# Attention by hash buckets and a gated feed-forward block on one core: aligned v blocks, full-height scores, a new order of loads, and one more pair turned by TensorE

## The chip, the core and the metric

The kernel runs on one core of a Trainium2 chip. A core has five engines that run side by side, each with its own instructions in order: TensorE (matmuls; PE in the profile, with PEld its weight loads), VectorE (DVE), ScalarE (ACT), GpSimd (POOL) and SyncE (SP, which here only issues DMAs). The metric is the time of one execution on the device in microseconds, the median of several runs.

## What is computed

There are 4 batches, 8 heads, 768 tokens and 64 dimensions per head. Every query and key is hashed to a 6-bit bucket by the signs of its product with `proj`, and a query attends only to keys of its own bucket:

```python
mask = q_bucket[:, :, :, None] == k_bucket[:, :, None, :]
scores = np.where(mask, scale * np.matmul(q, k.transpose(0, 1, 3, 2)), -1000000000.0)
attn = np.exp(scores - max); attn = attn / (sum + 1e-09); x = attn @ v
...
xn = x / rms * rms_g
out = (silu(xn @ w_gate) * (xn @ w_val)) @ w_out
```

The heads of a token are put side by side (512 wide, 3072 tokens); then come the normalization, the two products of width 1536, and the product back to 512.

## The kernel before

**Units and slots.** The work is cut into eight units `w`: batch `w // 2`, one half (384) of its queries, all eight heads. One slot `g` is one pair of key chunks (2 × 128 keys) of one head against a unit's 384 queries: two score matmuls (L348) into a bank pair of PSUM, and one exponential of 768 columns on ScalarE (`probs`, L358). Three slots make a head, six a pair of heads `hp`, 192 slots the whole attention. `SLOTS` is their order: for batches 0 and 1 it goes unit 0 pair 0, unit 1 pair 0, unit 0 pairs 1 to 3, unit 1 pairs 1 to 3; then units 2 and 3 in the same way (unit 2, pair 0, begins at slot 48; pair 1 of batch 1 at slot 60, pair 2 at 66, pair 3 at 72); units 4 to 7 one after the other.

**The order of everything else** is written by hand. `at(s, f, ..., rank)` puts a step into slot `s`; the loop at L731 issues, slot by slot, the next slot's scores, then the steps of the slot by rank. The engines don't wait for slots: each runs through its own instructions in the order of issue and waits only for data and buffers. A DMA queued on SyncE (`nc.sync`) therefore stands behind all that were queued on it earlier.

**The mask as extra rows.** The hash bits of q and k are added below the 64 rows of each head in the tile `QK` (fp16, 64 + 12 rows used), scaled such that a pair of different buckets falls out of the exponential. The score matmul therefore contracts over `KROWS` = 76 rows. The bits come from a hash (L214: four fp32 matmuls in one bank), a comparison on VectorE (`signs`, L221) and small DMAs on SyncE or copies that put them into rows 64 to 75 of `QK` (for a pair of batch 1, eight DMAs). `QK` has six buffers, in turn.

**Two ways to turn q and k.** The scores want the head dimension on partitions. A pair in `BY_PE` is loaded in rows (1536 bytes at a time, one DMA each for k and q), turned by TensorE in fp32 (`turn_pe`, L174, three turns per head and tensor), copied out by VectorE or ScalarE (`keep`, L182) and cast into `QK` by GpSimd or ScalarE (`cast_half`, L190). The other pairs are loaded by `load_blocks` in runs of 128 bytes (L126: four DMAs each for k and q), turned by VectorE in 32 × 32 blocks (`turn_dve`, L198, eight instructions per pair) and cast by GpSimd (`cast_pool`, L206). Before the change (0, 0) to (0, 3) and (1, 0) go the first way.

**v and the sums.** v is cast to fp16 into `vl` by GpSimd (`v_prep`, L314), in blocks of 66 values for each head and chunk: 64, a one that yields the sum of the exponentials, and one to spare. The `o_ps` matmuls (L370, `av`) read 65 columns of a block, with the exponentials as weights: 18 per head and unit, in two groups of nine. `v_sum` (L320 to L322, GpSimd) and `v_mean` (L329, TensorE) make a small correction, `cvb`. `attn_out` divides: `otmp` (L385) and `rcp` (L390) on VectorE, then the product (L394) and its square (L406) on GpSimd, or both on VectorE where `urgent`; `sumsq` (L410) sums the squares.

**The feed-forward block.** When a unit's eight heads are done, `norm` (L417 to L423, ending in `rstd` on GpSimd) gives the scale, `scale_x` the scaled rows `xn` in three chunks, `turn_x` their transposition into `xnT`. This is done by TensorE (L448, four matmuls per chunk, and a product on VectorE, L449), or, for the first two chunks of the units in `BY_DMA`, by DMA transposes on SyncE (L441). Then 12 times gate (L463), tanh on ScalarE (L465), value (L473), two products on VectorE (L474, L475), and three output chunks of 12 matmuls (`project`, L486). These steps of unit `w` start at slot `24 w + 42` and lie between the scores of later slots. The last output chunk is done apart, at the end (L742 to L759).

The weights are loaded by GpSimd's queue, with a cast (`load_w`, `load_wo`).

Of the kernel before, what the change touches and what calls it, by code (L numbers as in the profile page):

```python
# [8 lines left out]
FP32 = mybir.dt.float32  # L9
FP16 = mybir.dt.float16  # L10
# [5 lines left out]
H = 8  # L16
S = 768
D = 64
# [2 lines left out]
NF = DFF // 128  # L21
HALF = 384
KROWS = D + 12

TINY = 2.0e-38
QBIT = 16.0
# [11 lines left out]
LAST = {(w, h): g for g, (w, h, p) in enumerate(SLOTS) if p == 2}  # L38


BY_PE = [(0, hp) for hp in range(4)] + [(1, 0)]


BY_DMA = (3, 4, 5)


@with_exitstack
def kernel(
# [18 lines left out]
    qkpool = ctx.enter_context(tc.tile_pool(name="qkpool", bufs=6))  # L67
# [22 lines left out]
    wg = const.tile([128, 4, DFF], FP16, name="wg")  # L90
    wv = const.tile([128, 4, DFF], FP16, name="wv")
    wo = const.tile([128, NF, DMODEL], FP16, name="wo")
    vls = [const.tile([128, H, 6, 66], FP16, name=f"vl{i}") for i in range(2)]
    vsum = [const.tile([128, H, 66], FP16, name=f"vsum{i}") for i in range(2)]
    cvb = [const.tile([128, H, 66], FP32, name=f"cvb{i}") for i in range(2)]

    def bank(name, shape=None, dt=FP32):
# [33 lines left out]
    T0, QK = {}, {}  # L131

    def qk_tile(b, hp):
        if (b, hp) not in QK:
            QK[b, hp] = qkpool.tile([128, 2, 2 * S], FP16, name="QK")

    def t_tile(b, hp, which):
        T0[b, hp, which] = tpool.tile(
# [6 lines left out]

    def k_cols(b, h, jt):
        o = (jt // 3) * S + (jt % 3) * 128 if (b, h // 2) in BY_PE else S + jt * 128
        return QK[b, h // 2][0:KROWS, h % 2, o : o + 128]

    def q_cols(w, h):  # L150
        b, half = divmod(w, 2)
        t = QK[b, h // 2][0:KROWS, h % 2]
# [72 lines left out]
    def bit_rows(b, h, t):  # L225
        return QK[b, h // 2][D:KROWS, h % 2, t * HALF : (t + 1) * HALF]

# [50 lines left out]
    def hash_lone(b, hp):  # L278
# [57 lines left out]
    x, ssp, xn, xnT, ht = {}, {}, {}, {}, {}  # L336
# [41 lines left out]
    def attn_out(w, hp):  # L378
        b = w // 2
        if w not in x:  # L380
            x[w] = xpool.tile([128, 3, DMODEL], FP32, name="x")
            ssp[w] = xpool.tile([128, 3, 4], FP32, name="ssp")
        o = ot.pop((w, hp))
        tmp = spool.tile([128, 3, 2, 66], FP32, name="otmp")
        nc.vector.tensor_add(  # L385
            tmp[:, :, :, 0:65], o[:, :, :, 0:65],
            cvb[b % 2][:, 2 * hp : 2 * hp + 2, 0:65].unsqueeze(1).to_broadcast([128, 3, 2, 65]),
        )
        r = spool.tile([128, 3, 2, 1], FP32, name="rcp")
        nc.vector.reciprocal(r, tmp[:, :, :, 64:65])  # L390
        xd = x[w][:, :, 128 * hp : 128 * hp + 128]
        urgent = (w, hp) == (0, 3)
        eng = nc.vector if urgent else nc.gpsimd
        eng.tensor_mul(  # L394
            xd.rearrange("p c (h d) -> p c h d", h=2), tmp[:, :, :, 0:64],
            r.to_broadcast([128, 3, 2, 64]),
        )
        sq = spool.tile([128, 3, 128], FP32, name="sq")
        if urgent:
            for c in range(3):  # L400
                nc.vector.scalar_tensor_tensor(
                    out=sq[:, c], in0=xd[:, c], scalar=1.0, in1=xd[:, c],
                    op0=ALU.mult, op1=ALU.mult, accum_out=ssp[w][:, c, hp : hp + 1],
                )
        else:
            nc.gpsimd.tensor_mul(sq, xd, xd)  # L406
        return sq
# [124 lines left out]
    for i in range(2):  # L532
        nc.gpsimd.memset(vls[i][:, :, :, 64:65], 1.0)
        nc.gpsimd.memset(vsum[i][:, :, 64:65], 6.0)

    def load_w(dst, src, n0, n1):
        nc.gpsimd.dma_start(
# [57 lines left out]
    def at(s, f, *a, rank=3):  # L595
        plan[s].append((rank, len(plan[s]), lambda: f(*a)))
# [52 lines left out]
    at(27, v_prep, 1, 0)  # L649
    for h in range(2):  # L650
        at(41 + h, cast_half, 1, h, "q", 0)
    at(44, v_sum, 1, 0)
# [14 lines left out]
    for (b, hp), (loads, turns, cast_slots, sh) in work.items():  # L667
        for which, s in zip("kqv", loads):
            at(s, load_rows if which == "v" else load_blocks, nc.sync, b, hp, which)
        for i, s in enumerate(turns):  # L670
            at(s, turn_dve, b, hp, "kq"[i // 4], i % 4, rank=5)
        for which, s in zip("kq", cast_slots):
            at(s, cast_pool, b, hp, which)
        if sh:
            if b == 1:
                at(sh, hash_lone, b, hp)
            else:
                at(sh, hash_pairs, b, (hp - 1, hp))
# [22 lines left out]
    for w in range(8):  # L701
        for h in range(H):
            end = LAST[w, h] + (2 if (w, h) == (0, 7) else 3)
            at(end - 1, av, w, h, 0, 9)
            at(end, av, w, h, 9, 18)
            if h % 2:
                at(end, o_step, w, h // 2, rank=4.5)
                if (w, h) != (0, 7):
                    late = 3 if h == 7 and w < 6 else 5 if (w, h) == (0, 5) else 4
                    at(end + late, s_step, w, h // 2, rank=5 if late != 5 else 4)  # L710
        s0 = 24 * w + 42
        n0 = {0: 11, 2: 7, 3: 13, 4: 13, 5: 13}.get(w, 11)
        at(s0 - n0, norm, w, rank=5)
        for c in range(3):
            scale, rank = {0: 6, 2: 6 - c}.get(w, 8 - c), 1
            turn = {0: (4, 3, 2), 2: (4, 2, 1)}.get(w, (5, 3, 1))[c]
            if w in BY_DMA and c < 2:
                scale, turn, rank = 11 - c, 11 - c, 6
            at(s0 - scale, scale_x, w, c, rank=5)
            at(s0 - turn, turn_x, w, c, rank=rank)  # L720
        seen = set()
        for ft in range(NF):
            for f, s in ((g_step, s0 + 16 * ft // NF), (v_step, s0 + (32 * ft + 16) // (2 * NF))):
                at(s, f, w, ft, rank=4 if s in seen else 2)
                seen.add(s)
        for i in range(9 if w < 7 else 6):
            c, j = divmod(i, 3)
            at(s0 + 16 + i, project, w, c, 4 * j, 4 * j + 4, rank=1 if i == 8 else 3)


    for s in range(NS + 48):  # L731
# [3 lines left out]
        n = sum(r < 3 for r, _, _ in todo) if s < NS - 1 else 0  # L735
# [4 lines left out]
        for _, _, f in todo[n:]:  # L740
            f()
    rows = out[3 * S : 4 * S, :].rearrange("(p c) n -> p c n", c=6)[:, out_chunk(7, 2), :]  # L742
    for i in range(2):
        cs = slice(256 * i, 256 * i + 256)
        y = bank("y_ps")
        for ft in range(NF):
            nc.tensor.matmul(  # L747
                y[:, cs], ht[7][:, ft, 256:384], wo[:, ft, cs],
                start=(ft == 0), stop=(ft == NF - 1),
            )  # L750
        ysb = spool.tile([128, DMODEL], FP32, name="ysb", bufs=3)
        if i == 0:
            nc.scalar.copy(ysb[:, 0:256], y[:, cs])
            nc.sync.dma_start(out=rows[:, cs], in_=ysb[:, 0:256])
        else:
            nc.scalar.copy(ysb[:, 0:128], y[:, 256:384])
            nc.vector.tensor_copy(ysb[:, 128:256], y[:, 384:512])
            nc.scalar.dma_start(out=rows[:, 256:384], in_=ysb[:, 0:128])
            nc.sync.dma_start(out=rows[:, 384:512], in_=ysb[:, 128:256])  # L759


# [28 lines left out]
```

## Time and profile before

| | |
|---|---|
| median of 3 runs | 334.26 us (334.0 to 335.18) |
| span of the profiled execution, first to last instruction | 332.5 us |
| time of the profiled execution beside its span | not given; the median of the runs is 1.8 us above the span |
| TensorE busy | 323.3 us (97%) |
| VectorE, ScalarE, GpSimd busy | 234.2, 208.0, 157.1 us |
| mean granted clock of TensorE | 0.998 of full speed |
| DMA | 32.41 MB in 89956 packets, 75336 of them under 512 bytes |

The profile gives, for every group of equal instructions, the engine, the line, the tiles, the shapes, the count, the busy time and the mean of one, and what ended the idle time before them. A timeline row gives the start, the length, and in brackets the idle time ahead of it with its releaser. Matmuls overlap in the array, so the length of one (325 ns for a score) is more than the distance of two starts (162 ns); distances of starts are what TensorE's time is made of. The chain of work that ended last is followed back from the last instruction.

### The profile page before, as it was taken

How to read it: one execution, taken by the hardware profiler on the slowest of the kernel's cores; microseconds unless marked ns; L12 is line 12 of the kernel's file. 1: busy time of each engine (PE TensorE's matmuls, PEld its weight loads, DVE VectorE, ACT ScalarE, POOL GpSimd, SP SyncE). 2: the span in 40 equal slices, each digit the busy share in tenths (PEclk: the TensorE clock that was granted, in tenths of full speed). 3: DMA queues.
4: the chain of work that ended last, by engine and by line, in shares of the span. 5: the costliest groups of instructions: out<-in, count | busy, mean ns of one | idle time of the engine just before them, and what ended most of it. 6: DMA issues, size and time to landing. Idle time of an engine off the chain costs nothing.

```text
span 332.5 us, 7788 instructions
## 1 busy us (share of the span) xinstructions
PE 323.3 (97%) x2959; PEld 198.5 (60%) x2959; DVE 234.2 (70%) x526; ACT 208.0 (63%) x324; POOL 157.1 (47%) x230
## 2 busy tenths in 40 slices
PE   8999989998999999999999999999999999999995
PEld 7576656555566556656565656566566656655653
DVE  3799579997598956989476874977257753793860
ACT  3788977674576665667675766757666766422421
POOL 4887956487747476376744365643110311130000
PEclk9999999999999999999999999999999999999999
DMA  6995997898348927841361714000200001002002
GB/s 221 349 201 151 147 173 140 158 172 134 117 86 156 168 40 174 156 90 24 91 146 34 141 34 150 3 17 18 80 32 2 3 32 65 0 3 82 13 2 95
DMA packets 89956, 32.41 MB, mean 97 GB/s; under 512 B 75336, under 2 KB 86848, under 8 KB 89920
## 3 DMA queue, kind: packets, MB, share of 16 engines
q1 hardware_dynamic: 85984, 27.14, 35.0%
q0 software_dynamic: 3712, 4.72, 9.2%
q8 instruction: 23, 0.38, 0.5%
q14 instruction: 13, 0.11, 0.1%
q10 hardware_dynamic: 224, 0.07, 0.1%
HBM read 28.58 MB, written 6.29 MB: 105 GB/s over the span
## 4 chain that ended last, share of the span: by engine, by line
PE 82%; DVE 5%; DMA 5%; POOL 4%; ACT 1%; issue 1%; SPq 1%; POOLq 0%; DVEq 0%; ACTq 0%
PE v_ps L473 17%; PE y_ps L486 16%; PE s_ps L348 15%; PE g_ps L463 14%; PE o_ps L370 9%; PE s_ps L463 4%; PE d_ps L214 3%; DMA QK<-bits 3%; PE t_ps L174 2%; DMA kL<-in_k_dram 1%; PE z_ps L341 1%; PE x_ps L448 1%; DVE t L474 1%; PE y_ps L747 1%; POOL sq L406 1%
## 5 line engine op out<-in xcount | busy, mean ns | idle before, releaser
L358 ACT ACTIVATE psb<-s_ps 128x768 f16<-128x768 f32 x192 | 150.6, 809 | 31.9 <-PE s_ps L348 29.9
L348 PE MATMUL s_ps<-QK 76*128 76x384 f16 x384 | 93.7, 325 | 2.5 <-DMA QK<-bits 1.3
L473 PE MATMUL v_ps<-xnT,wv 128*128 128x384 f16 x384 | 78.1, 325 | 0.0
L486 PE MATMUL y_ps<-wo,ht 128*128 128x512 f16 x276 | 69.2, 378 | 0.0
L394 POOL TENSOR_TENSOR x<-otmp,rcp 128x384 f32<-128x384 f32 x31 | 26.1, 843 | 84.8 <-DVE rcp L390 84.6
L370 PEld LDWEIGHTS <-psb 128*128 128x128 f16 x1152 | 52.2, 97 | 22.0 <-issue 3.6
L465 ACT ACTIVATE t<-g_ps 128x384 f32<-128x384 f32 x78 | 38.3, 491 | 43.2 <-PE g_ps L463 42.7
L463 PE MATMUL g_ps<-xnT,wg 128*128 128x384 f16 x312 | 63.4, 325 | 0.3
L474 DVE SCALAR_TENSOR_TENSOR t<-t,g_ps 128x384 f32<-128x384 f32 x78 | 42.7, 547 | 28.8 <-ACT t L465 28.4
L475 DVE SCALAR_TENSOR_TENSOR ht<-t,v_ps 128x384 f16<-128x384 f32 x96 | 53.2, 554 | 10.4 <-PE v_ps L473 0.9
L370 PE MATMUL o_ps<-vl,psb 128*128 128x65 f16 x1152 | 56.7, 193 | 0.3 <-DVE otmp L385 0.3
L463 PEld LDWEIGHTS <-wg 128*128 128x128 f16 x384 | 36.0, 97 | 24.1 <-issue 0.7
L473 PEld LDWEIGHTS <-wv 128*128 128x128 f16 x384 | 36.2, 97 | 23.2
L348 PEld LDWEIGHTS <-QK 76*128 76x128 f16 x384 | 31.3, 98 | 19.3 <-issue 4.7
L486 PEld LDWEIGHTS <-ht 128*128 128x128 f16 x276 | 26.0, 97 | 26.3 <-issue 1.9
L493 ACT COPY ysb<-y_ps 128x512 f32<-128x512 f32 x23 | 13.5, 587 | 24.6 <-PE y_ps L486 24.1
L406 POOL TENSOR_TENSOR sq<-x 128x384 f32<-128x384 f32 x31 | 26.3, 849 | 2.4
L385 DVE TENSOR_TENSOR otmp<-o_ps,cvb 128x390 f32<-128x390 f32 x32 | 17.9, 559 | 12.6 <-PE o_ps L370 12.5
L206 POOL CAST QK<-qT 64x768 f16<-64x768 f32 x22 | 18.1, 823 | 15.8 <-DVE qT L198 15.1
L206 POOL CAST QK<-kT 64x768 f16<-64x768 f32 x22 | 18.5, 841 | 13.6 <-PE m_ps L329 3.8
L449 DVE TENSOR_TENSOR xnT<-x_ps,gcol 128x512 f16<-128x512 f16 x18 | 12.2, 683 | 14.1 <-PE x_ps L448 14.0
L198 DVE STREAM_TRANSPOSE kT<-kL 128x192 f32<-128x192 f32 x44 | 21.7, 515 | 0.0
(81 smaller groups left out, 297.6 us busy)
## 6 DMA issues: line engine op xcount, KB each, us to landing
vL<-in_v_dram SPq DMA_DIRECT2D x16, 384.0 KB
out_dram<-ysb SPq DMA_DIRECT2D x23, 256.0 KB
kL<-in_k_dram SPq DMA_DIRECT2D x44, 96.0 KB
qL<-in_q_dram SPq DMA_DIRECT2D x44, 96.0 KB
kL<-in_k_dram SPq DMA_DIRECT2D x4, 384.0 KB
qL<-in_q_dram SPq DMA_DIRECT2D x4, 384.0 KB
wg<-in_moe_w_gate_dram POOLq DMA_DIRECT2D x2, 768.0 KB, 8.2
wv<-in_moe_w_val_dram POOLq DMA_DIRECT2D x2, 768.0 KB, 9.3
```

The costliest lines, as they stand in the source:

```text
L206: nc.gpsimd.tensor_copy(QK[b, hp][0:64, hh, o : o + S], T0[b, hp, which][64 * hh : 64 * hh + 64, :])
L348: nc.tensor.matmul(ps[:, j, 0:HALF], k_cols(w // 2, h, 2 * p + j), q_cols(w, h), start=True, stop=True,)
L358: nc.scalar.activation(psb[w, h][:, p], sps.pop(g)[:, :, 0:HALF], AF.Exp, scale=ESCALE,)
L370: nc.tensor.matmul(o[:, c, hh, 0:65], psb[w, h][:, jt // 2, jt % 2, 128 * c : 128 * c + 128], vls[b % 2][:, h, v_chunk(b, h, jt), 0:65], s ...
L394: eng.tensor_mul(xd.rearrange("p c (h d) -> p c h d", h=2), tmp[:, :, :, 0:64], r.to_broadcast([128, 3, 2, 64]),)
L406: nc.gpsimd.tensor_mul(sq, xd, xd)
L463: nc.tensor.matmul(g, wg[:, kt, fs], xnT[w][:, kt], start=(kt == 0), stop=(kt == 3))
L465: nc.scalar.activation(t, g, AF.Tanh, scale=0.5)
L473: nc.tensor.matmul(vv, wv[:, kt, fs], xnT[w][:, kt], start=(kt == 0), stop=(kt == 3))
L474: nc.vector.scalar_tensor_tensor(out=t, in0=t, scalar=1.0, in1=g, op0=ALU.add, op1=ALU.mult)
L475: nc.vector.scalar_tensor_tensor(out=ht[w][:, ft], in0=t, scalar=0.5, in1=vv, op0=ALU.mult, op1=ALU.mult)
L486: nc.tensor.matmul(y, ht[w][:, ft, c * 128 : (c + 1) * 128], wo[:, ft, :], start=(ft == 0), stop=(ft == NF - 1),)
```

## The change

- **Blocks of 144 bytes.** The step of a v block goes from 66 to 72 fp16 values.
- **Scores over 128 rows** for (1, 0), (1, 1) and all pairs of batches 2 and 3. The six `QK` buffers become fixed tiles, and rows 64 to 127 of each are set to zero by GpSimd before the first use of this kind: buffers 4 and 5 at the start, 2 and 3 in slots 76 and 78, 0 and 1 in slots 97 and 98.
- **Pair (1, 1) by TensorE.** It joins `BY_PE`: loaded in rows (slot 16; v at 29), turned in slots 29, 31, 33 and 35, hashed at slot 40 instead of 51; its last casts come at 45 and 47.
- **Order.** (1, 2) and (1, 3) are loaded, turned and hashed seven slots earlier (k and q loads at 27, 28 and 31, 34; hashes at 51 and 58); k of (1, 3) is queued at slot 31, before the bits of (1, 0) at 33. The v work of (2, 1) moves two slots later. Two `v_mean` move four slots earlier. In unit 0 pair 2 is now `urgent` too. Unit 6's normalization moves two slots earlier, and one of its `sumsq` one slot.
- **Unit 6** joins `BY_DMA`.
- **The tail.** The last chunk is made in three pieces (256, 128, 128 columns), each with its own tile and one copy, instead of two pieces of 256, the second copied by two engines.

```diff
+VSTEP = 72
...
-BY_PE = [(0, hp) for hp in range(4)] + [(1, 0)]
-BY_DMA = (3, 4, 5)
+BY_PE = [(0, hp) for hp in range(4)] + [(1, 0), (1, 1)]
+BY_DMA = (3, 4, 5, 6)
...
-    vls = [const.tile([128, H, 6, 66], FP16, name=f"vl{i}") for i in range(2)]
+    vls = [const.tile([128, H, 6, VSTEP], FP16, name=f"vl{i}") for i in range(2)]
+    qkbuf = [const.tile([128, 2, 2 * S], FP16, name=f"QK{i}") for i in range(6)]
...
-            QK[b, hp] = qkpool.tile([128, 2, 2 * S], FP16, name="QK")
+            QK[b, hp] = qkbuf[len(QK) % len(qkbuf)]
+    def clear_rows(i):
+        nc.gpsimd.memset(qkbuf[i][D:128].rearrange("p h n -> p (h n)").bitcast(FP32), 0.0)
+    def score_rows(b, hp):
+        return slice(0, 128 if (b, hp) in ((1, 0), (1, 1)) or b > 1 else KROWS)
...
-        return QK[b, h // 2][0:KROWS, h % 2, o : o + 128]
+        return QK[b, h // 2][score_rows(b, h // 2), h % 2, o : o + 128]
...
-        urgent = (w, hp) == (0, 3)
+        urgent = (w, hp) in ((0, 2), (0, 3))
...
+    clear_rows(4)
+    clear_rows(5)
...
-    for which, sl in zip("kqv", (9, 11, 15)):
-        at(sl, load_rows, nc.sync, 1, 0, which)
-    for i, sl in enumerate((20, 21, 24, 27)):
-        at(sl, keep_pair, 1, 0, i)
-        at(sl + 1, casts, 1, 0, i)
-    at(33, hash_pair, 1, 0)
...
+    for hp, loads, turns, sh, evens, sv in (
+        (0, (9, 11, 15), (20, 21, 24, 27), 33, (41, 42), (27, 44)),
+        (1, (16, 16, 29), (29, 31, 33, 35), 40, (45, 47), (49, 51)),
+    ):
+        for which, sl in zip("kqv", loads):
+            at(sl, load_rows, nc.sync, 1, hp, which)
+        for i, sl in enumerate(turns):
+            at(sl, keep_pair, 1, hp, i)
+            at(sl + 1, casts, 1, hp, i)
+        at(sh, hash_pair, 1, hp)
...
-        (1, 1): in_row((21, 22, 32), 42, 51), (1, 2): in_row((34, 35, 37), 49, 58),
-        (1, 3): in_row((38, 40, 44), 56, 65),
+        (1, 2): in_row((27, 28, 38), 42, 51), (1, 3): in_row((31, 34, 45), 49, 58),
...
-        at(cast_slots[2], v_prep, b, hp)
-        at(cast_slots[2], v_sum, b, hp)
+        late = 2 if (b, hp) == (2, 1) else 0
+        at(cast_slots[2] + late, v_prep, b, hp)
+        at(cast_slots[2] + late, v_sum, b, hp)
         if b > 1 and hp % 2:
-            at(48 * b + (17 if hp == 3 else -4), v_mean, b, hp - 1, 4)
+            at(48 * b + (17 if hp == 3 else -8), v_mean, b, hp - 1, 4)
...
+    for i, s in ((2, 76), (3, 78), (0, 97), (1, 98)):
+        at(s, clear_rows, i, rank=6)
...
-                if (w, h) != (0, 7):
-                    late = 3 if h == 7 and w < 6 else 5 if (w, h) == (0, 5) else 4
-                    at(end + late, s_step, w, h // 2, rank=5 if late != 5 else 4)
+                if (w, h) not in ((0, 5), (0, 7)):
+                    late = 3 if h == 7 and w < 7 else 4
+                    at(end + late, s_step, w, h // 2, rank=5)
...
-        n0 = {0: 11, 2: 7, 3: 13, 4: 13, 5: 13}.get(w, 11)
+        n0 = {0: 11, 2: 7, 3: 13, 4: 13, 5: 13, 6: 13}.get(w, 11)
...
-    for i in range(2):
-        cs = slice(256 * i, 256 * i + 256)
+    for lo, hi in ((0, 256), (256, 384), (384, 512)):
...
+        copy, queue = (nc.vector.tensor_copy, nc.sync) if hi == 512 else (nc.scalar.copy, nc.scalar)
+        copy(ysb[:, lo:hi], y[:, lo:hi])
+        queue.dma_start(out=rows[:, lo:hi], in_=ysb[:, lo:hi])
```

More of the change, by code (lines that the diff above doesn't have):

```diff
@@ L66 @@
     tpool = ctx.enter_context(tc.tile_pool(name="tpool", bufs=2))
-    qkpool = ctx.enter_context(tc.tile_pool(name="qkpool", bufs=6))
     ppool = ctx.enter_context(tc.tile_pool(name="ppool", bufs=3))
@@ L147, in k_cols @@
         o = (jt // 3) * S + (jt % 3) * 128 if (b, h // 2) in BY_PE else S + jt * 128
-        return QK[b, h // 2][0:KROWS, h % 2, o : o + 128]
+        return QK[b, h // 2][score_rows(b, h // 2), h % 2, o : o + 128]
     def q_cols(w, h):
         b, half = divmod(w, 2)
-        t = QK[b, h // 2][0:KROWS, h % 2]
+        t = QK[b, h // 2][score_rows(b, h // 2), h % 2]
         if (b, h // 2) in BY_PE:
@@ L640 @@
     at(78, load_grow)
-    for which, sl in zip("kqv", (9, 11, 15)):
-        at(sl, load_rows, nc.sync, 1, 0, which)
-    for i, sl in enumerate((20, 21, 24, 27)):
-        at(sl, keep_pair, 1, 0, i)
-        at(sl + 1, casts, 1, 0, i)
-    at(33, hash_pair, 1, 0)
[L649 to L652, printed above, removed]
+    for hp, loads, turns, sh, evens, sv in (
[8 more added lines that the diff above has]
+        at(sh, hash_pair, 1, hp)
+        for hh, sl in enumerate(evens):
+            at(sl, cast_half, 1, 2 * hp + hh, "q", 0)
+        at(sv[0], v_prep, 1, hp)
+        at(sv[1], v_sum, 1, hp)
     def in_row(loads, s, hash_slot=None):
@@ L747 @@
             nc.tensor.matmul(
-                y[:, cs], ht[7][:, ft, 256:384], wo[:, ft, cs],
+                y[:, lo:hi], ht[7][:, ft, 256:384], wo[:, ft, lo:hi],
                 start=(ft == 0), stop=(ft == NF - 1),
@@ L751 @@
         ysb = spool.tile([128, DMODEL], FP32, name="ysb", bufs=3)
[L752 to L759, printed above, removed]
+        copy, queue = (nc.vector.tensor_copy, nc.sync) if hi == 512 else (nc.scalar.copy, nc.scalar)
+        copy(ysb[:, lo:hi], y[:, lo:hi])
+        queue.dma_start(out=rows[:, lo:hi], in_=ysb[:, lo:hi])
 _INS = ['q', 'k', 'v', 'proj', 'moe_w_gate', 'moe_w_val', 'moe_w_out', 'moe_rms_g']
```

## The prediction

> **What bounds the kernel now.** I read the page first, then the engines by stretch, TensorE's timeline around each hole, SyncE's queue, and the chain.
>
> ```profile
> span 332.5 us, 7788 instructions
> ...
> PE 323.3 (97%) x2959; PEld 198.5 (60%) x2959; DVE 234.2 (70%) x526; ACT 208.0 (63%) x324; POOL 157.1 (47%) x230
> ```
>
> TensorE works 323.3 of 332.5 us and takes its instructions in order, so there are two ways to save: cheaper or fewer matmuls, and fewer holes. These are the holes that the change can reach (start, duration, engine, line, idle before it and who ended it):
>
> ```profile
> 44.26 0.49 PE L348 MATMUL s_ps<-QK 76*128 76x384 f16 x2
> 45.36 0.40 PE L448 MATMUL x_ps<-ident,xn 128*128 128x128 f16 x4 [0.61 <-DVE xn L434]
> ...
> 47.47 0.43 PE L370 MATMUL o_ps<-vl,psb 128*128 128x65 f16 x9 [0.34 <-DVE otmp L385]
> ...
> 76.65 0.48 PE L348 MATMUL s_ps<-QK 76*128 76x384 f16 x2 [0.94 <-DMA QK<-bits]
> ...
> 121.10 0.40 PE L448 MATMUL x_ps<-ident,xn 128*128 128x128 f16 x4 [0.59 <-DVE xn L434]
> 121.33 1.03 PE L486 MATMUL y_ps<-wo,ht 128*128 128x512 f16 x4
> ...
> 131.91 0.45 PE L370 MATMUL o_ps<-vl,psb 128*128 128x65 f16 x9
> 132.50 0.81 PE L463 MATMUL g_ps<-xnT,wg 128*128 128x384 f16 x4
> ```
>
> A pair of scores holds TensorE 0.33 us, four `x_ps` turns 0.23 (121.10 to 121.33) and nine `o_ps` 0.29 (below). The first hole is therefore 45.36 − 44.26 − 0.33 = 0.77, which is 0.16 more than the idle time printed (that counts from a modelled end); with 0.16 added the others are 0.50 at 47.0, 1.10 at 75.6 (pair (1,1)'s bits) and 0.75 at 120.4. The last is 132.50 − 131.91 − 0.29 = 0.30.
>
> The bits come through SyncE's queue, which has a backlog:
>
> ```profile
> 32.43 6.44 SPq L126 DMA_DIRECT2D kL<-in_k_dram  x4
> 38.98 7.11 SPq L126 DMA_DIRECT2D qL<-in_q_dram  x4
> 46.19 1.76 SPq L116 DMA_DIRECT2D vL<-in_v_dram  x1
> 48.05 7.05 SPq L272 DMA_DIRECT2D QK<-bits  x8
> 55.20 2.71 SPq L126 DMA_DIRECT2D kL<-in_k_dram  x4
> ```
>
> Pair (1,1)'s k and q hold the queue from 32.43 to 46.1; (1,0)'s bits (48.05) wait behind them, although they are queued at slot 33, fifteen slots before their use.
>
> **The change, part by part.**
>
> *144-byte blocks of v.* The trace shows the `o_ps` matmuls that read them:
>
> ```profile
> 163.04 0.45 PE L370 MATMUL o_ps<-vl,psb 128*128 128x65 f16 x9
> 163.33 0.33 PE L348 MATMUL s_ps<-QK 76*128 76x384 f16 x1
> ...
> L370 PE MATMUL o_ps<-vl,psb 128*128 128x65 f16 x1152 | 56.7, 193 | 0.3 <-DVE otmp L385 0.3
> ```
>
> Nine start within 0.29 us, 32 ns apart. Record by record they are 29, 35, 33, 32, 29, 33, 29, 33 and 33 ns apart: after the first, whose surplus falls on the second, the fast ones are those whose block begins at a multiple of 16 bytes. With a step of 132 bytes that is every fourth block, with 144 every block. Over the inner records of all 1152 the means are 29.2 ns (begin on 16) and 32.2 (others), 31.5 together. So (31.5 − 29.2) × 1152 = 2.65 us, of which 882 records lie behind slot 48: 2.0 us there, 0.65 before, where ScalarE sets the pace in part; I count half, 0.3. The bounds are 0 and 2.65.
>
> The Trainium skill, "TensorE: Matmul & The Clock Gate", section "Back-to-back issue gap", gives the warm gap by columns alone (N/2.4 + 2.5 ns; 29.6 for 65, an estimate by that page), wherever the operand begins. By that rule the padding brings nothing; the trace agrees only for blocks that begin on 16, so the measurement decides. The rule is a rival below.
>
> *128-row scores.* A score matmul over 76 rows and a gate matmul over 128 take the same:
>
> ```profile
> L348 PE MATMUL s_ps<-QK 76*128 76x384 f16 x384 | 93.7, 325 | 2.5 <-DMA QK<-bits 1.3 <-ACT psb L358 0.8 <-ACT qT L182 0.2
> ...
> L463 PE MATMUL g_ps<-xnT,wg 128*128 128x384 f16 x312 | 63.4, 325 | 0.3
> ...
> masks.py:197 POOL MEMSET ident<- 128x128 f32 x1 | 0.2, 204 | 0.3 <-POOLq L774 0.3
> ...
> L518 POOL MEMSET pq<- 128x48 f32 x1 | 0.1, 149 | 0.0
> ```
>
> Zero, then, within a rounding of 1 ns on 240 matmuls (0.24 us either way). The price is six clears of 1536 words on GpSimd. 80 words more cost 55 ns, so one takes 0.15 + 1488 × 0.69 ns = 1.2 us (4.8 by the small row alone). Two come at the start, where GpSimd is idle before its first cast:
>
> ```profile
> 5.51 1.06 POOL L190 CAST QK<-kT 64x384 f16<-64x384 f32 x2 [2.10 <-DVE kT L182]
> ...
> 113.01 0.83 POOL L394 TENSOR_TENSOR x<-otmp,rcp 128x384 f32<-128x384 f32 x1 [4.31 <-DVE rcp L390]
> ```
>
> 2.4 us against 2.1 idle: that cast is 0.3 late, and the first scores wait for the bits anyway. Two fall in or before the 4.31 us gap ahead of 113.01, the last two behind unit 2's normalization. Nothing on TensorE; without that cover up to 1 us.
>
> *Pair (1,1) by TensorE.* Added: 12 fp32 turns in slots 29 to 35; the hash moves from slot 51 to 40, those of (1,2) and (1,3) from 58 and 65 to 51 and 58.
>
> ```profile
> 30.72 0.49 PE L174 MATMUL t_ps<-ident,kL 128*128 128x128 f32 x3
> 31.05 0.43 PE L370 MATMUL o_ps<-vl,psb 128*128 128x65 f16 x9
> ...
> 40.26 0.48 PE L348 MATMUL s_ps<-QK 76*128 76x384 f16 x2 [0.30 <-ACT psb L358]
> ...
> 41.46 0.50 PE L348 MATMUL s_ps<-QK 76*128 76x384 f16 x2
> ```
>
> Three turns take 0.33, so +1.32. A hash with its preamble takes 1.20 − 0.33 = 0.87: +0.87 ahead of slot 48, −0.87 behind it. ScalarE sets the pace in slots 29 to 36 and TensorE waits for it (0.30 at 40.26), which hides some 0.4. VectorE swaps eight transposes in slots 42 to 63 for four copies in 29 to 35, a relief where it is full.
>
> Unit 0's chain: (0,2)'s product and squares move from GpSimd to VectorE, which today waits for GpSimd's squares (first row of the fence below: 1.54). I take half of that as gained, 0.8 us, since (0,2)'s own work and the added copies now stand on VectorE in its place (bounds 0 and 1.54); so of the holes at 44.6 and 47.0 I count 1.0 of 1.27.
>
> ```profile
> 40.63 0.55 DVE L410 TENSOR_REDUCE ssp<-sq 128x3 f32<-128x384 f32 x1 [1.54 <-POOL sq L406]
> ...
> 56.20 0.49 PE L348 MATMUL s_ps<-QK 76*128 76x384 f16 x2
> ...
> 53.00:54.00 1.00, 1.00 (x8) 0.60 (x7) 0.90 (x3) 0.72 (x3) 0.00 (x0) 1.00 0.47 130
> ...
> 57.00:60.00 3.00, 3.00 (x28) 1.91 (x26) 2.90 (x8) 2.44 (x5) 1.00 (x2) 1.00 0.80 126
> ```
>
> TensorE would then reach slot 48 (56.20 now, the first score of (1,0) in unit 2) at 56.2 + 1.32 + 0.87 − 0.4 − 1.0 − 0.3 = **56.7**.
>
> *SyncE's queue.* (1,1)'s rows need two issues near 28 us instead of eight block loads; but (1,2)'s eight take exactly that place at 32.43, and (1,3)'s k, four more, is queued ahead of (1,0)'s bits (slot 31 before 33). Now the v load stops flowing about 53.5 (DMA share 0.47 in 53 to 54, last but one column), and the bits land right behind it, before 56.2. Four block loads flow in about 3.0 us (57 to 60 at 126 GB/s is 0.38 MB; four are 0.39). So the first bits flow at 56.5 and land about 1 us later (an estimate between 0 and the 2.4 us from the last output's issue, below, to the span's end): **57.5**. TensorE waits 0.8 us there: a new hole, slot 48 at 57.5 instead of 56.2, +1.3. Behind TensorE's wait stand unit 0's gate matmuls, and ScalarE and VectorE behind those.
>
> The later bits have room: (1,1)'s eight, after q of (1,3), are issued about 63 to 69, some 7 us ahead of slot 60 (76.65). The hole of 1.10 goes.
>
> *Changes of order.* (2,1)'s v work leaves the way of unit 2's rstd:
>
> ```profile
> 116.45 0.82 POOL vl L314
> ...
> 119.66 0.87 POOL rstd L423
> ```
>
> Of the 3.2 us from 116.45 to 119.66 all but rstd's own first step (0.2) is that work, far more than the hole of 0.75: it goes. `v_mean` four slots earlier leaves the crowded banks: 0.30. *Unit 6's turns* by DMA: 8 of TensorE's, 2 × 0.23 = 0.46; ten slots of lead hide the DMAs. *The tail:*
>
> ```profile
> 329.08 0.27 ACT L756 COPY ysb<-y_ps 128x128 f32<-128x128 f32 x1 [0.94 <-PE y_ps L747]
> ...
> 329.38 0.29 DVE L757 COPY ysb<-y_ps 128x128 f32<-128x128 f32 x1 [7.06 <-ACT ysb L756]
> 329.70 0.33 SPq L759 DMA_DIRECT2D out_dram<-ysb  x1
> ```
>
> The last copy no longer stands behind ScalarE's: 0.30.
>
> **The sum.** +1.3 up to slot 48; behind it −0.87 (hash) − 2.0 (blocks) − 1.10 − 0.75 − 0.30 − 0.46 − 0.30 = −5.8. About 0.5 of that will be eaten by waits on VectorE, which is busy for 2.90 of the 3.00 us of 57 to 60 above. Net −4.0: span 332.5 to 328.5. The page gives no other time of the profiled execution than its span; the median of the runs (334.26) is 1.8 us above it, and I leave that as it is: **330.3 us**.
>
> **The rivals.**
>
> 1. *The bits come in time.* If k of (1,3) flows in the gaps of the weights, slot 48 starts at 56.7: 0.8 us less, and with nothing eaten 1.3 less, 329.0. For it: 54 to 56 is nearly idle now. Against it: one ring, in order.
>
> 2. *The padding does nothing* (the page's rule as a mechanism: the gap is set by the columns): 2.3 us more, 332.6. Against it: the split of 29.2 and 32.2 goes with the offset alone.
>
> 3. *Slower: the bits of (1,0) land far too late.* k of (1,3) is issued while `wo` flows. If its four loads are held as q's were (7.11 for four), the queue comes to the bits at 47.95 + 7.1 = 55.1, and if these land like those whose wait the chain shows, 5.53 after their issue, it is 62:
>
> ```profile
> 1.04 3.17 PE z_ps L341 x28
> 4.21 1.28 PE t_ps L174 x6
> ...
> 70.99 5.53 DMA QK<-bits
> ```
>
> A hole of 5 us: +4.5 on my sum. After a long rest TensorE also runs at half pace: at the start six turns take 1.28 us, where three take 0.33 later, and 28 matmuls of 128 columns 3.17, where four take 0.23. That pace holds from 1.04 to 5.49 at least, so it would cost 2 us more: 336.8. It decides from about 61 us on. The Trainium skill, same page, section "HAM oscillation — how this bites in real kernels", puts the bound at idle gaps over about 3.4 us; no row here has such a gap behind the start, so the trace can't show it.
>
> 4. *New waits* of the same size as the old ones (GpSimd's casts and clears, VectorE's (0,2) work ahead of its copies): 2 to 3 us more, 333.
>
> **How the numbers follow.** Forecast 0.47 (329.2 to 331.8 for it alone), rival 1 0.19, 2 0.08, 3 0.12, 4 0.14. Half a per cent is 1.67 us, about what a measurement of this kernel can tell from no change (the three runs span 1.2). Faster means under 332.6: the forecast, rival 1, half of rival 2 and a third of rival 4, 0.75. Slower, over 335.9: most of rival 3 and a rest, 0.12. Between, 0.13. The range begins at rival 1 with its bounds: 329.0 less 0.35 (blocks in full), 0.27 (early holes in full), 0.24 (rows) and 0.9 (the turns wholly hidden), 327.2. It ends at 334.6, beyond rival 4 and short of rival 3.
>
> **What would show it.** Right: `o_ps` groups of nine in 0.265 us; no hole at 75.6 and 120.4; a hole at slot 48 marked by bits; SyncE's row for (1,0)'s bits at 51 or later; eight `x_ps` turns fewer. Wrong: nine `o_ps` still in 0.29; no hole at slot 48; a hole there over 3 us, with turns or scores at half pace behind it; new idle rows on `s_ps` between 5 and 35 us.

## The result, and the profile after

| | before | after |
|---|---|---|
| median of 12 runs each, us | 333.97 (332.70 to 336.28) | 336.62 (333.55 to 339.39) |
| ratio after / before | | 1.0056, 95% interval 1.0031 to 1.0081 |
| span of the profiled execution, us | 332.5 | 331.6 |

The kernel became slower by 0.56%; 330.3 us and a gain were forecast. (The ratio leaves out the two slowest runs of after, 338.81 and 339.39 us, which lie over 1.5% above its fastest, and it is not the quotient of the two medians, 1.008.) The profiled execution of after is the fastest of its 12 runs, 333.55 us, and one of the two in which TensorE kept its full clock throughout; so the profile shows most of where the time went, but not all.

The page of after, its head and three groups:

```profile
span 331.6 us, 7854 instructions
PE 320.6 (97%) x2975; PEld 198.5 (60%) x2975; DVE 236.2 (71%) x526; ACT 208.2 (63%) x324; POOL 165.3 (50%) x238
...
L355 PE MATMUL s_ps<-QK 128*128 128x384 f16 (+1 forms) x384 | 93.7, 326 | 3.8 <-DMA QK<-bits 1.9
...
L493 PE MATMUL y_ps<-wo,ht 128*128 128x512 f16 x276 | 69.4, 379 | 2.1 <-DMA wo<-in_moe_w_out_dram 2.1
...
L377 PE MATMUL o_ps<-vl,psb 128*128 128x65 f16 x1152 | 56.0, 193 | 0.0
```

(The lines of TensorE's rows here are 7 higher in after than in before; others have moved by other amounts.) TensorE is busy for 2.7 us less. Two idle times stand against that: 1.9 us on the bits, which was forecast (0.8), and 2.1 us on `wo`, which was not. In the page of before the same group has no idle time:

```profile
L486 PE MATMUL y_ps<-wo,ht 128*128 128x512 f16 x276 | 69.2, 378 | 0.0
```

TensorE's timeline in after shows both:

```profile
55.34 0.81 PE L480 MATMUL v_ps<-xnT,wv 128*128 128x384 f16 x4
58.03 0.48 PE L355 MATMUL s_ps<-QK 128*128 128x384 f16 x2 [1.87 <-DMA QK<-bits]
...
77.56 0.59 PE L493 MATMUL y_ps<-wo,ht 128*128 128x512 f16 x2
80.29 0.59 PE L493 MATMUL y_ps<-wo,ht 128*128 128x512 f16 x2 [2.13 <-DMA wo<-in_moe_w_out_dram]
...
131.72 0.44 PE L377 MATMUL o_ps<-vl,psb 128*128 128x65 f16 x9
132.00 0.49 PE L355 MATMUL s_ps<-QK 76*128 76x384 f16 x2
```

By distances of starts, as in the prediction, the holes are 2.04 us (slot 48, at 58.03 instead of 57.5) and 2.29 us (80.29 − 77.56 − two `y_ps` of 0.22). The old holes at 75.6, 120.4 and 132.2 are gone. Nine `o_ps` take 0.28 us (131.72 to 132.00), 0.01 less than before, not 0.02 less.

SyncE's queue, where (1,3)'s k stands ahead of (1,0)'s bits:

```profile
31.70 7.99 SPq L127 DMA_DIRECT2D kL<-in_k_dram  x4
39.79 7.17 SPq L127 DMA_DIRECT2D qL<-in_q_dram  x4
47.06 0.59 SPq L117 DMA_DIRECT2D vL<-in_v_dram  x1
47.75 6.99 SPq L127 DMA_DIRECT2D kL<-in_k_dram  x4
54.84 6.19 SPq L279 DMA_DIRECT2D QK<-bits  x8
```

The four loads at 47.75 are held for 6.99 us, as q's were (7.17), so the bits are issued from 54.84 on. The trace has the second of the eight landing at 57.89, and slot 48 starts 0.14 us later (0.14 again in two other profiled runs, after landings at 57.98 and 58.48). In those two the profile puts the wait down to casts on GpSimd that ended beside the landing; in after the same casts ended behind the start of slot 48 (58.12 and later), so slot 48 does not wait for them.

The hole on `wo` comes from GpSimd. First its timeline in before, then in after:

```profile
67.81 0.46 POOL L321 TENSOR_TENSOR vadd<-vadd 128x128 f32<-128x128 f32 x1
68.35 0.46 POOL L322 TENSOR_TENSOR vsum<-vadd 128x128 f16<-128x128 f32 x1
68.75 0.89 POOL L543 DMA_DIRECT2D wo<-in_moe_w_out_dram  x1
```

```profile
67.68 1.00 POOL L327 TENSOR_TENSOR vadd<-vL 128x384 f32<-128x384 f32 x1
...
69.29 0.45 POOL L329 TENSOR_TENSOR vsum<-vadd 128x128 f16<-128x128 f32 x1
69.69 0.82 POOL L321 CAST vl<-vL 128x768 f16<-128x768 f32 x1
...
72.08 0.46 POOL L329 TENSOR_TENSOR vsum<-vadd 128x128 f16<-128x128 f32 x1
72.48 0.89 POOL L552 DMA_DIRECT2D wo<-in_moe_w_out_dram  x1
```

GpSimd issues the load of `wo`'s second half (`load_wo` in slot 52) in order with its casts and sums. The change makes slots 49 to 51 hold the v work of two pairs, (1,1) and (1,2); the load starts at 72.48 instead of 68.75 and lands at 80.24 instead of 77.34. TensorE wants it for the third `y_ps` behind slot 60: at 77.99 in after, and at 77.41 in before (76.98 and two of 0.22), where it came with 0.07 us to spare:

```profile
76.98 1.03 PE L486 MATMUL y_ps<-wo,ht 128*128 128x512 f16 x4
```

### The profile page after: what moved, and what is told of

Same layout as the page of the kernel before. It is cut to its first block, busy times and chain, and to the rows that moved or that the text cites. A ratio compares the mean times of both kernels' runs of the same rounds, so it can differ in the third digit from the quotient of the medians.

```text
span 331.6 us, 7854 instructions
## 1 busy us (share of the span) xinstructions
PE 320.6 (97%) x2975; PEld 198.5 (60%) x2975; DVE 236.2 (71%) x526; ACT 208.2 (63%) x324; POOL 165.3 (50%) x238
## 4 chain that ended last, share of the span: by engine, by line
PE 88%; DVE 4%; DMA 4%; ACT 2%; POOL 1%; issue 1%; DVEq 0%; ACTq 0%; POOLq 0%
PE y_ps L493 18%; PE s_ps L355 18%; PE v_ps L480 17%; PE g_ps L470 14%; PE o_ps L377 10%; PE d_ps L221 4%; PE s_ps L470 4%; DMA wo<-in_moe_w_out_dram 2%; PE t_ps L181 2%; ACT psb L365 1%; PE x_ps L455 1%; PE z_ps L348 1%; DMA QK<-bits 1%; DMA out_dram<-ysb 1%; DVE t L481 1%
## 5 line engine op out<-in xcount | busy, mean ns | idle before, releaser
L355 PE MATMUL s_ps<-QK 128*128 128x384 f16 (+1 forms) x384 | 93.7, 326 | 3.8 <-DMA QK<-bits 1.9
L377 PE MATMUL o_ps<-vl,psb 128*128 128x65 f16 x1152 | 56.0, 193 | 0.0
L355 PEld LDWEIGHTS <-QK 128*128 128x128 f16 (+1 forms) x384 | 31.0, 98 | 20.0 <-issue 3.4
L413 POOL TENSOR_TENSOR sq<-x 128x384 f32<-128x384 f32 x30 | 25.6, 852 | 2.4
L213 POOL CAST QK<-qT 64x768 f16<-64x768 f32 x20 | 16.7, 837 | 14.9 <-DVE qT L205 12.2
L213 POOL CAST QK<-kT 64x768 f16<-64x768 f32 x20 | 17.0, 849 | 14.4 <-DVE kT L205 12.5
L456 DVE TENSOR_TENSOR xnT<-x_ps,gcol 128x512 f16<-128x512 f16 x16 | 10.8, 683 | 14.0 <-PE x_ps L455 14.0
L205 DVE STREAM_TRANSPOSE kT<-kL 128x192 f32<-128x192 f32 x40 | 19.8, 519 | 0.0
```

Of the source, the lines that this page charges most:

```text
L213: nc.gpsimd.tensor_copy(QK[b, hp][0:64, hh, o : o + S], T0[b, hp, which][64 * hh : 64 * hh + 64, :])
L355: nc.tensor.matmul(ps[:, j, 0:HALF], k_cols(w // 2, h, 2 * p + j), q_cols(w, h), start=True, stop=True,)
L377: nc.tensor.matmul(o[:, c, hh, 0:65], psb[w, h][:, jt // 2, jt % 2, 128 * c : 128 * c + 128], vls[b % 2][:, h, v_chunk(b, h, jt), 0:65], s ...
```

## The experiments

**The two orders mended.** The first kernel is the changed one with two edits: (1,3)'s k queued behind (1,0)'s bits again, and `wo`'s second half issued in slot 51 ahead of the v work. The next two have one edit each.

```diff
# e1_both: both; e2_bits: the first alone; e3_wo: the second alone
-        (1, 2): in_row((27, 28, 38), 42, 51), (1, 3): in_row((31, 34, 45), 49, 58),
+        (1, 2): in_row((27, 28, 38), 42, 51), (1, 3): in_row((34, 34, 45), 49, 58),
...
-        at(36 + 16 * i, load_wo, 6 * i, 6 * i + 6)
+        at(36 + 15 * i, load_wo, 6 * i, 6 * i + 6, rank=3 - i)
```

> The changed kernel with both of its new holes taken away: k of (1,3) is queued behind the bits of (1,0) (slot 34 instead of 31), and the second half of wo is loaded in slot 51, ahead of the v work of (1,1) and (1,2) on GpSimd, instead of slot 52 behind it. Theory (the two holes of 2.0 and 2.3 us cost their own length, and in most runs a stretch of TensorE at half clock besides): no hole over 0.8 us, clock 1.0 in all runs, span 331.6 - 4.3 = 327.3, up to 328.5 if small waits come back; time about 329.5, 1.3% under the kernel before. Rival (the lower clock comes from something else, such as scores over 128 rows): span 4 us shorter but the clock still 0.990 to 0.995 in most runs, time 331 to 333.

> Only k of (1,3) queued behind the bits of (1,0). Theory: the hole at slot 48 goes, the one at the wo load stays (2.3 us, perhaps up to 4 since TensorE gets there sooner). One hole is left that can bring the half clock: the clock is 0.995 in some runs, 1.0 in the others, time 331 to 334. Rival (the hole at slot 48 alone sets the clock): 1.0 in all runs, 331.5. Rival (something else): 0.990 to 0.995 as in the changed kernel, 334.

> Only the second half of wo loaded in slot 51, ahead of the v work. Theory: the hole in the output product goes, the one at slot 48 stays (2.0 us); clock 0.995 in some runs, time 331.5 to 334. Rival (the hole at the wo load alone sets the clock): 1.0 in all runs, 331.5.

| | median, us | ratio to before, 95% | hole left in the trace |
|---|---|---|---|
| both | 329.62 (329.30 to 330.38) | 0.9873, 0.9849 to 0.9896 | none over 0.70 |
| bits alone | 332.21 (331.05 to 333.84) | 0.9941, 0.9919 to 0.9964 | 2.08 on `wo` |
| `wo` alone | 332.06 (331.46 to 334.48) | 0.9953, 0.9933 to 0.9973 | 2.83 at slot 48 |

With both edits SyncE's queue, GpSimd and TensorE read (three views):

```profile
47.38 8.61 SPq L279 DMA_DIRECT2D QK<-bits  x8
56.09 2.70 SPq L127 DMA_DIRECT2D kL<-in_k_dram  x4
```

```profile
65.95 0.89 POOL L552 DMA_DIRECT2D wo<-in_moe_w_out_dram  x1
```

```profile
55.57 0.81 PE L480 MATMUL v_ps<-xnT,wv 128*128 128x384 f16 x4
56.22 0.49 PE L355 MATMUL s_ps<-QK 128*128 128x384 f16 x2
```

The bits go first again and the same four loads take 2.70 us behind them; `wo` is issued 6.5 us sooner; slot 48 follows `v_ps` without a gap. So the two queued transfers were the whole loss: with both mended the change gains 1.27%, and no other version here is faster. The two edits bring 7.0 us off the changed kernel's median (336.62), while the two holes of its profile add up to 4.3. So the holes cost more than their own length; why is the next question.

**The clock.** The changed kernel was run again beside the others, this time with the clock caught falling.

> The changed kernel once more, unaltered, beside the others of this call. Theory: two holes of 2 us or more, at slot 48 (bits) and in unit 0's output product (wo); most runs at a mean clock of 0.995 or less, median 335.5 to 337. If the profiled run is one of these, its trace shows scores or gates at half pace (over 0.3 us from start to start instead of 0.162) for 3 to 4 us right behind one of the two holes. Rival (the clock falls elsewhere): the half pace lies somewhere without a hole.

335.63 us (333.91 to 338.90), ratio 1.0059, 1.0034 to 1.0085. Its busy times by stretch (columns: stretch, its length, busy time and count of PE, PEld, DVE, ACT, POOL, granted clock, DMA share, GB/s):

```profile
55.57:58.98 3.41, 1.35 (x10) 0.66 (x8) 2.14 (x5) 0.79 (x2) 3.29 (x6) 1.00 0.30 49
58.98:62.40 3.42, 3.42 (x21) 1.90 (x20) 1.11 (x3) 1.95 (x3) 0.37 (x1) 0.50 0.05 14
...
79.47:82.88 3.41, 1.46 (x16) 0.78 (x15) 2.06 (x3) 0.81 (x1) 3.29 (x5) 1.00 1.18 181
82.88:86.29 3.41, 3.41 (x13) 1.58 (x12) 0.45 (x1) 2.21 (x3) 1.62 (x3) 0.50 0.91 142
```

and the same in the profiled run of after, which kept its clock, around its first and its second hole:

```profile
55.07:58.48 3.41, 1.54 (x17) 0.89 (x16) 2.71 (x6) 1.19 (x2) 3.21 (x6) 1.00 0.64 66
58.48:61.89 3.41, 3.41 (x31) 2.21 (x29) 1.99 (x5) 2.60 (x5) 0.97 (x2) 1.00 0.05 14
...
78.96:82.37 3.41, 2.08 (x19) 1.18 (x19) 0.85 (x2) 0.81 (x1) 3.21 (x5) 1.00 0.81 131
82.37:85.79 3.42, 3.42 (x39) 2.16 (x38) 1.19 (x3) 2.11 (x3) 0.49 (x2) 1.00 0.84 134
```

Behind each of the two holes of the first run (2.22 and 2.11 us) TensorE ran for 3.413 us at half clock, with 21 and 13 matmuls in a stretch where after at full clock has 31 and 39; each such stretch costs half of 3.413, 1.7 us. The stretches lie on a fixed grid: the clock's changes in every profiled run are whole multiples of 3.413 us apart (here 16 of them at full clock, one at half, 6 full, one half, 73 full). What seems to count is how much of a hole falls within one step of the grid. In the 13 profiled runs of this case, no step at full clock with up to 2.04 us without a matmul was followed by half clock, and all three with 2.11 us or more (2.11, 2.22 and 3.24) were. In after's second hole the grid cut the 2.29 us in two (0.97 and 1.32), in the run with `wo` alone mended 2.83 us (1.13 and 1.70), and nothing happened. One more step was followed by half clock, but it had itself been at half clock: below, in the run without pair (1,1), it had 2.02 us without a matmul and went on at half pace. The place of the bound between 2.04 and 2.11 us thus rests on few steps, all at full clock.

The runs agree. By their mean clock (a step at half is 3.413 × 0.5 / 335 = 0.005):

| kernel | over 0.997 | 0.993 to 0.995 (one step) | 0.990 or less (two) |
|---|---|---|---|
| after, 24 runs of two series | 3 | 12 | 9 |
| one hole (bits alone and `wo` alone), 24 runs | 18 | 6 | 0 |
| no hole (both), 6 runs | 6 | 0 | 0 |
| before, 75 runs beside the others | 72 | 2 | 1 |

In the second series of after the run without such a step took 333.91 us, the median of six with one was 335.3 and of five with two 337.4: 1.4 and 3.5 us more. The kernel before, whose profile has no hole over 1.2 us behind its first scores, shows the lower clock in 3 of 75 runs; none of these three was profiled, so why is open.

**The holes filled.** The changed kernel, with matmuls of ones (128 columns, 37 and 42 of them) put ahead of the scores of slots 48 and 60, so that TensorE is busy while it waits:

```diff
-        idle(ps[:, 0, HALF:512], {0: 8, 3: 6}.get(g, 0))
+        idle(ps[:, 0, HALF:512], {0: 8, 3: 6, 48: 37, 60: 42}.get(g, 0))
```

> The changed kernel with both holes kept but filled: 37 matmuls of ones (128 columns, 55 ns each, 2.0 us) ahead of the scores of slot 48 and 42 (2.3 us) ahead of those of slot 60; their results are overwritten. Theory (idle TensorE makes the clock fall): the span stays at the changed kernel's best, 331.6 to 332.6, but the clock is 1.0 in every run, so that the median falls from 336.6 to about 334. Rival (the clock falls for another reason): clock 0.990 to 0.995 in most runs and the median stays at 336 to 337.

334.40 us (333.43 to 338.58), ratio 1.0015, 0.9989 to 1.0041, with the clock over 0.997 in 11 of 12 runs. TensorE's timeline at slot 48:

```profile
55.65 2.23 PE L348 MATMUL s_ps<-ones 128*128 128x128 f16 x37
58.12 0.49 PE L355 MATMUL s_ps<-QK 128*128 128x384 f16 x2 [0.24 <-DMA QK<-bits]
```

Slot 48 starts no sooner (58.12), yet the kernel gains 1.4 us by the ratios (1.0015 against 1.0056 and 1.0059) and 1.2 to 2.2 by the medians: the wait is the same, the half clock behind it is gone. (Three runs took 335.7 to 336.4 us at full clock, up to 3.0 us more than the fastest, so the clock is not all that varies.)

**A hole alone.** The kernel before with `wo`'s second half two slots later, and nothing else:

```diff
-        at(36 + 16 * i, load_wo, 6 * i, 6 * i + 6)
+        at(36 + 18 * i, load_wo, 6 * i, 6 * i + 6)
```

> The kernel before, with one thing: the second half of wo is loaded in slot 54 instead of 52, so that it lands some 2.5 us later and unit 0's output product has to wait. Nothing else of the change is in it. Theory (a hole costs its length and, in part of the runs, a stretch at half clock): span 334 to 335 with the clock at 1.0 in some runs, 0.995 or less in others, median 336 to 338 against 334.2. Rival (other parts of the change pull the clock down): 1.0 in all runs and the length of the hole alone, 335.5 to 336.5.

335.43 us (334.25 to 339.62), ratio 1.0045, 1.0021 to 1.0069; five of 12 runs at a clock of 0.995 or less. TensorE's timeline:

```profile
75.25 0.59 PE L486 MATMUL y_ps<-wo,ht 128*128 128x512 f16 x2
77.55 0.59 PE L486 MATMUL y_ps<-wo,ht 128*128 128x512 f16 x2 [1.70 <-DMA wo<-in_moe_w_out_dram]
```

By the starts the hole is 1.86 us (77.55 − 75.25 − 0.44). The profiled run kept its clock, and none of the five that lost it was profiled; that their holes were longer is not shown. Beside them 29 of 29 runs of the kernel before kept theirs. So none of the change's new matmuls or rows is needed for it: the late load alone makes the hole and lowers the clock. It also took something away: the old hole at slot 60 is gone in this trace, where (1,1)'s bits were issued from 66.65 on and `wo`'s load at 69.77 (in before from 69.29 on, and at 68.75).

**Pair (1,1) left as it was.** The changed kernel without (1,1) in `BY_PE`, and with the loads and hashes of (1,1), (1,2) and (1,3) of before:

```diff
-BY_PE = [(0, hp) for hp in range(4)] + [(1, 0), (1, 1)]
+BY_PE = [(0, hp) for hp in range(4)] + [(1, 0)]
...
-        (1, (16, 16, 29), (29, 31, 33, 35), 40, (45, 47), (49, 51)),
...
-        (1, 2): in_row((27, 28, 38), 42, 51), (1, 3): in_row((31, 34, 45), 49, 58),
+        (1, 1): in_row((21, 22, 32), 42, 51), (1, 2): in_row((34, 35, 37), 49, 58),
+        (1, 3): in_row((38, 40, 44), 56, 65),
```

> The changed kernel with pair (1,1) loaded, turned and hashed as before, and the loads of (1,2) and (1,3) as before; the rest of the change stays. Theory: neither new hole (the queue and GpSimd's v work are as before), the old hole of 1.1 at slot 60 stays; what is left of the change brings what the traces give for it: blocks 1.3, scores 0.4, unit 6 0.5, order 0.8 to 1.2, tail 0.3, sum 3.3 to 3.7; clock 1.0 in all runs, median about 330.7. Rival (the parts that stay are worth little or cost something): 333 to 336.

332.76 us (330.01 to 336.74), ratio 0.9945, 0.9919 to 0.9971: the expectation of no new hole was a miss. The clock was over 0.997 in four of 12 runs only. TensorE's timeline and the stretches on the grid of the profiled one (336.28 us):

```profile
73.67 0.44 PE L377 MATMUL o_ps<-vl,psb 128*128 128x65 f16 x9
79.21 0.80 PE L355 MATMUL s_ps<-QK 128*128 128x384 f16 x2 [5.10 <-DMA QK<-bits]
```

```profile
73.78:77.19 3.41, 0.33 (x10) 0.21 (x7) 2.34 (x5) 0.00 (x0) 3.21 (x5) 1.00 1.00 211
77.19:80.60 3.41, 1.39 (x4) 0.58 (x5) 1.81 (x3) 0.49 (x1) 2.44 (x4) 0.50 0.05 15
80.60:84.02 3.42, 3.42 (x18) 1.64 (x17) 0.00 (x0) 1.13 (x2) 0.00 (x0) 0.50 0.83 131
```

The old hole at slot 60, 1.10 us in before, has grown to 5.26: TensorE arrives 1.6 us sooner (73.9), and (1,1)'s first bits, issued at 71.10, land at 78.68, where before they were issued at 69.29, behind the same loads, and landed at 75.49. `wo`'s second half is issued at 67.66 here, 1.1 us sooner than before, ahead of the last of these loads; that it holds them and the bits was not tried by itself, though the trace of the late load above fits it. The profiled run is one of the slowest of the twelve, and without its two steps at half clock it would still take 332.9 us, where the fastest, at full clock, took 330.01; so the hole is hardly as long in each. So in that run, without the early hash of (1,1), a faster TensorE ran into late bits; how often that happens the runs don't tell.

**The single terms,** each undone in the version with both orders mended, or done alone in the kernel before:

```diff
# e5_step66: blocks back to 132 bytes
-VSTEP = 72
+VSTEP = 66
# e9_rows76: all scores over 76 rows
-        return slice(0, 128 if (b, hp) in ((1, 0), (1, 1)) or b > 1 else KROWS)
+        return slice(0, KROWS)
# e10_pool02: (0,2) on GpSimd again, its sumsq where it was
-        urgent = (w, hp) in ((0, 2), (0, 3))
+        urgent = (w, hp) == (0, 3)
# e11_align: the kernel before, with blocks of 144 bytes
-    vls = [const.tile([128, H, 6, 66], FP16, name=f"vl{i}") for i in range(2)]
+    vls = [const.tile([128, H, 6, 72], FP16, name=f"vl{i}") for i in range(2)]
```

> The changed kernel with both new holes mended (as in e1_both, 329.6) and the v blocks back at a step of 132 bytes. My prediction's figure for the blocks: 2.3 us more, 331.9. By the changed kernel's trace, where the gap of the o_ps matmuls fell only to 30.7 ns and not to 29.2: 0.9 to 1.3 us more, 330.5 to 330.9. Rival (the padding does nothing, the gap is set by the columns): 329.6 as it is.

> The version with both orders mended, with every score back to 76 rows (the clears of the buffers stay). By the prediction the rows cost and bring nothing: 329.6 us, as with 128 rows, within 0.3. The rival reads the slots in the two traces: between slots 96 and 138, where no hole was removed, six slots take 0.06 us less than in the kernel before, and the blocks of v explain only half of that (0.03 per six slots in the run with a step of 66); if the rows are the other half, the kernel loses about 0.6 to 0.9 us, 330.2 to 330.5, and each pair of scores starts its second matmul 2 to 3 ns later.

> The version with both orders mended, with pair 2 of unit 0 back as before: its product and squares on GpSimd, its sum of squares where it was. The prediction counted 1.0 us for the move to VectorE, through the holes at 44.6 and 47.0. If it was worth that, 330.6 us, with a hole of 0.5 us or more between slots 39 and 45. The rival: with the chain of unit 0 made earlier by other steps or covered by other work, it is worth under 0.3: 329.6 to 329.9.

> The kernel before with the blocks of v at 144 bytes and nothing else. By the prediction's term, -2.65 us at most and about -2.0 with holes eating some: 331.7 to 332.2. By the run that took the blocks back (0.2 us in the times, 0.6 between slots 72 and 191 in the trace, 10 ns for nine matmuls instead of 20): 333.2 to 334.0, hardly to be told from no change.

| | median, us | ratio to before, 95% |
|---|---|---|
| both orders, for comparison | 329.62 | 0.9873, 0.9849 to 0.9896 |
| blocks back | 329.82 | 0.9870, 0.9850 to 0.9890 |
| rows back | 329.86 | 0.9864, 0.9830 to 0.9897 |
| (0,2) back | 330.48 | 0.9884, 0.9850 to 0.9917 |
| before with 144-byte blocks | 333.49 | 0.9968, 0.9944 to 0.9992 |

*Blocks.* The runs put them at 0.2 us, or 1.1 with an interval from 0.3 to 1.9. In the traces their gain between slots 72 and 191 is 0.57 us (144 against 132 bytes in the mended version), and 0.5 from slot 78 to the end (before with and without). The spans of those two profiles of before differ by 1.0 us, but the rest of that lies in how soon the first scores began (7.76 against 8.83 us). That is not the blocks' doing: with `wo` late, where the kernel is the same up to there, they began at 7.95.

*Rows.* The times don't tell 128 from 76. In the traces a pair of scores takes 162.5 + 162.5 ns from start to start over 128 rows and 166.5 + 161.7 over 76; 3.2 ns for 120 slots are 0.4 us, which the slots show too (0.36 from slot 57 to the end). So the rival had the mechanism, at half of its size.

*(0,2).* With it on GpSimd the kernel takes 0.86 us more, and all of it falls in one place: up to slot 39 that run is 0.32 us ahead of the mended version, from slot 42 on 0.66 behind. Its timeline there:

```profile
44.44 0.48 PE L355 MATMUL s_ps<-QK 76*128 76x384 f16 x2
45.67 0.40 PE L455 MATMUL x_ps<-ident,xn 128*128 128x128 f16 x4 [0.74 <-DVE xn L441]
```

That is the hole that stood at 44.6 in before.

## Why the prediction was wrong

**The missing step: GpSimd's queue.** The sum followed the moved loads along SyncE's queue and put GpSimd's clears into its idle gaps. It left out that pulling (1,2) and (1,3) seven slots forward also moves their v work, four GpSimd instructions each, and that (1,2)'s now stands ahead of a DMA. The load of `wo`'s second half had 0.07 us of slack, and the hole of 1.10 at 75.6, which the sum took away, was part of what covered it. The 3.7 us later issue became a hole of 2.29. The mended order and the late load by itself both show it. Rival 4 had waits of this size (2 to 3 us, from GpSimd's casts and clears), but not this one: no sum of the prediction has `wo`'s load in it.

**The step with the wrong bound: the half clock.** The sum put the half clock at nothing. Rival 3 had the mechanism, half pace behind a hole on the bits, but asked for a hole of 5 us and let it decide from slot 48 at 61 us on. The holes that came were 2.0 to 2.3 us, slot 48 began near 58, and the clock fell in 21 of 24 runs, for 1.7 us a step; 30 steps in 24 runs are 2.1 us on average. The bound of about 3.4 us that was cited from the Trainium skill, "TensorE: Matmul & The Clock Gate", section "HAM oscillation — how this bites in real kernels", is too lax for this kernel: 2.11 us were enough. Part 1 of the same page says that the window of 3413 ns runs freely, and the grid of 3.413 us agrees. That a hole shorter than one window can be enough, if it falls within one, is what the runs showed.

**The mis-sized term: blocks of 144 bytes.** Forecast 2.65 us (2.0 behind slot 48), measured 0.5 to 0.6 in the traces. The step that failed is that aligned blocks would all go at 29.2 ns. They do not: in after most inner `o_ps` are 29 ns apart, but the one behind the second and the one behind the seventh of each nine come 34 ns apart, and the mean is 30.7 (31.5 before). The 35 ns behind the second stood in the prediction's own list, where it was put down to the first's surplus; it is there with aligned blocks as well. What sets these two gaps no run here tells. Rival 2, that the columns set the pace, was nearer for this term. The formula that the prediction cites beside it is given in the Trainium skill, "TensorE: Matmul & The Clock Gate", section "Back-to-back issue gap", for a matmul by itself; of a stream of weight loads and matmuls, as it is here, that section says that both set the spacing. From the first of nine to the start of what follows them the mended version takes 274.6 ns with blocks of 144 bytes and 281.6 with 132 (means over the groups with no wait behind them). Those 7 ns, for the 79 groups between slots 72 and 191, are 0.55 us, so all of it reaches the slots.

**SyncE's queue: right.** The bits were issued at 54.84 (51 or later in the forecast, 55.1 in rival 3), and the first two landed at 57.7 and 57.9 (57.5 in the forecast, 62 in rival 3). What was off is the hole, 2.04 instead of 0.8: slot 48 began 0.5 later than forecast, and TensorE got there 0.7 sooner (its `v_ps` are through at 55.99, where the forecast had 56.7).

**The rest: nearly right.** In the mended version, which has neither of the two holes, the terms can be read from the starts of the slots against before:

| | forecast, us | measured, us |
|---|---|---|
| from slot 0 to 48, without the queue | +0.5 | +0.49 |
| slots 48 to 72: hash and bits of (1,1) | −1.97 | −2.09 |
| hole at 120.4 | −0.75 | −0.51 |
| hole at 132.2 | −0.30 | −0.38 |
| unit 6 by DMA | −0.46 | −0.51 |
| tail | −0.30 | 0.0 |
| (0,2) on VectorE (in the first row) | −1.0 | −0.98 |

The first row's agreement is luck in part. With `wo` late, where nothing is changed ahead of slot 48, the same stretch is 0.26 us longer than in before, because that run began 0.88 us sooner and lost part of it again; the mended version began 0.47 sooner.

The tail's copy starts 0.2 us sooner behind the last matmul (0.76 us to the last issue instead of 0.97), but from that issue to the end of the span it takes 3.0 us instead of 2.8. Not foreseen was a second hole of 0.31 at 207.8 that the earlier `v_mean` removed as well (0.48 in the slots), and a start of the first scores 0.47 us sooner. The latter is no gain of the change: the 13 profiles have it between 7.76 and 8.83 us, the latest in the profile of before, where TensorE also came to its full clock last (7.07 us).

From the forecast span of 328.5 to the 331.6 of the profiled run: +0.5 at slot 48, +2.3 for `wo`, +1.4 for the blocks, +0.3 for the tail, less 0.5 that nothing ate, 0.5 for the second `v_mean` and 0.4 for the rows, makes 3.1, as was measured. The half clock lies on top of that in the runs: 330.3 + 3.1 + 2.1 is 335.5, against medians of 336.62 and 335.63. The profile is that of the fastest run of its series, so the holes of the others may be longer; no run here shows it.

## What to carry to other kernels

When a step is moved, follow everything that it issues on every queue, and look for the transfer with no slack that stands behind it there; here it was one weight load among GpSimd's casts. In this kernel a hole in a busy TensorE cost its own length up to about 2 us; from there on it could cost 1.7 us more, in a share of the runs, so one good profile may hide it: look at the clocks of all runs. If such a wait can't be removed, matmuls without use that fill it can give the second part back, as they did here.

## What the runs showed of the hardware

- The half clock comes in steps of 3.413 us on a grid that is fixed within a run; the first change came 3.8 to 7.1 us after the first instruction, another time in each profiled run. A step at full clock that had 2.11 us or more without a matmul was followed by one at half (three of three); 2.04 us did not do it. A step that was itself at half clock was followed by another with 2.02 us.
- An `o_ps` matmul of 65 columns over a block that begins at a multiple of 16 bytes follows its neighbour in 29 ns, but not five times in a row: about every fifth takes 34.
- The same score matmul takes 3.2 ns less per pair over 128 rows than over 76 (162.5 + 162.5 against 166.5 + 161.7 ns), though both have a duration of 325 to 326 ns in the groups.
- A group of four block loads on SyncE's queue took 2.70 us to issue in the mended version and 6.99 in after, where GpSimd's load with a cast was flowing (47.3 to 53.0 us); that the one holds the other was not tried by itself.
